# Retention, then a gated linear unit: queries turned as single bf16 tokens or as four-byte words of two

## The chip, the cores and the metric

The kernel runs on one core of one Trainium2 chip. A core has five engines that run side by side, each through its own list of instructions in order: PE (matrix products, with its weight loads shown apart as PEld), DVE (vector), ACT (scalar), POOL (GpSimd) and SP, which here only starts DMAs. They meet through semaphores. The metric is the device time of one run in microseconds (us); lower is better.

## The reference

There are 8 batches, 8 heads, 576 tokens and 64 elements a head. The first half is retention: attention without softmax, with a decay per head.

```python
scores = scale * np.matmul(q, k.transpose(0, 1, 3, 2))
gamma = 1.0 - 2.0 ** (-5.0 - np.arange(H, dtype=np.float32))
Dmat = np.where(rel >= 0, gamma[:, None, None] ** rel[None, :, :], 0.0)
x = np.matmul(scores * Dmat, v)        # then heads side by side: (B, S, 512)
```

The second half takes that x, runs a causal convolution of five taps per channel, and gates a linear layer with it.

```python
gate = 1.0 / (1.0 + np.exp(-causal_conv(x, conv_w)))
out = (gate * (x @ w_val)) @ w_out
```

## The kernel before

The work is cut into 36 chunks of 128 tokens: four full ones for each batch, and after every four batches two "tail" chunks that hold the last 64 tokens of two batches each. The decay is folded into the values (a factor per token, L221) and into the result (L331), so that a chunk needs: scores of keys against queries (`scores`, L273), a product with a causal mask (`masks`, L286), values times masked scores (`values`, L313), plus queries times the state that earlier chunks left (`carried`, L295), and the state's update (`update`, L342, copied out by `take_state`, L356). Two chunks together make a unit for the second half: convolution as products with diagonal matrices (`conv`, L378), `gate`, `value` and `project` (L391 to L420).

PE contracts over partitions, so keys and queries, which arrive with tokens on the partitions, have to be turned: head elements go onto the partitions. For each group of 128 columns (two heads) PE multiplies the data with an identity in its transpose mode and writes the turned tile into PSUM; a copy takes it from there to SBUF. `turn_k` does that for keys, `turn_q` for queries.

Queries of a batch are loaded at once (`load_queries`, L105) as float32, four consecutive tokens to a partition: 128 partitions, 8 heads, 4 tokens `r`, 64 elements. A query job `("batch", b, r)` takes one `r`: `cast_q` (L228) makes it bf16 with 512 elements a partition (POOL, unless another engine is named), and `turn_q` (L252) turns its four groups and copies the result to one quarter of the tile `qtb` of that batch. The tokens of a chunk are therefore ordered by `r` first, and the mask `mask_q` (L160) is stored in that order. Queries of tail chunks have jobs of their own, `("own", t)`.

The order is written out by hand. Each engine runs its instructions in the order in which the program's calls name them. From L448 to L540 stands a prologue for the first chunks; batch 0 is cast at L457 and turned at L461 to L463, batch 1 at L519 and L528 to L531. `keep_warm` issues products that no result uses. Then a loop over slots (L542 to L597): slot `t` loads ahead, casts values for `t + 2` and queries for the jobs of `t + 1`, computes the scores of `t + 1` and the values of `t`, and does half of a unit's second part: convolution and `value` in even slots, `project` in odd ones. The turns of a query job stand between the two `value` or `project` calls (L584), a second job of the same slot after them (L591). Which slot has which job is in `qjobs` (L425 to L432): batch 2 in slots 5 and 6, two jobs each, later batches one job in each of the last four free slots before they are needed.

Turned keys and queries share one PSUM tile, `tps` (pool `ps_t`, one buffer). The prologue also uses tiles `g` of the pool `ps_g`, which has three buffers and otherwise serves the second half.

Of the kernel before, what the change touches and what calls it, by code (L numbers as in the profile page):

```python
# [13 lines left out]
F32 = mybir.dt.float32  # L14
BF16 = mybir.dt.bfloat16
# [6 lines left out]
def kernel(  # L22
# [10 lines left out]
    nc = tc.nc  # L33
    B, H, S, D = q.shape
    DM = moe_w_val.shape[0]
    KC = moe_conv_w.shape[0]
    P = 128
    NP = H // 2
# [5 lines left out]
    RQ = NCH  # L44
# [4 lines left out]
    consts = ctx.enter_context(tc.tile_pool(name="c", bufs=1))  # L49
    half = ctx.enter_context(tc.tile_pool(name="half", bufs=2))  # L50
    bfp = ctx.enter_context(tc.tile_pool(name="bfp", bufs=4))
# [5 lines left out]
    ps_t = ctx.enter_context(tc.tile_pool(name="pst", bufs=1, space=PSUM))  # L57
# [3 lines left out]
    ps_g = ctx.enter_context(tc.tile_pool(name="psg", bufs=3, space=PSUM))  # L61


    chunks = []
# [6 lines left out]
    with tc.manual_schedule():  # L71

        loaded = {}
# [17 lines left out]
        def load_keys(t):  # L91

            kind, b, c = chunks[t]
            kb = bfp.tile([P, H, D], BF16, name="kb", bufs=LA + 3)
            if kind == "full":
                nc.gpsimd.dma_start(out=kb, in_=k[b, :, c * P:(c + 1) * P, :].rearrange("h p d -> p h d"))  # L96
            else:
                for i in range(2):
                    nc.gpsimd.dma_start(out=kb[i * TAIL:(i + 1) * TAIL],
                                        in_=k[b + i, :, c * P:S, :].rearrange("h p d -> p h d"))  # L100
            kbf[t] = kb
# [9 lines left out]
        cwn = consts.tile([KC * NP, P], F32, name="cwn")  # L111
# [30 lines left out]
        for h in range(H):  # L142
# [5 lines left out]
        ident = consts.tile([P, P], BF16, name="ident")  # L148
        nc.gpsimd.memset(ident, 1.0)
        nc.gpsimd.affine_select(ident, ident, pattern=[[-1, P]], base=0, channel_multiplier=1,  # L150
                                compare_op=ALU.is_equal, fill=0.0)

        mask = consts.tile([P, P], BF16, name="mask")
        nc.gpsimd.memset(mask, 1.0)
# [28 lines left out]
        nc.vector.memset(sbd[1], 0.0)  # L183
        for t in xg:
            nc.vector.memset(t[:, :, :, 0:PAD], 0.0)
        identf = consts.tile([32, 32], F32, name="identf")
        nc.vector.tensor_copy(identf, ident[0:32, 0:32])
        id2 = consts.tile([P, 64], F32, name="id2")
        nc.vector.tensor_tensor(id2, ident[:, 0:64], ident[:, 64:128], op=ALU.add)
        mask_t = consts.tile([P, P], BF16, name="maskt")  # L190
# [4 lines left out]

        def prep_conv_weights():
            cps = ps_t.tile([P, KC * NP], F32, name="tps")
            nc.tensor.transpose(cps, cwn, identf[0:KC * NP, 0:KC * NP])
            nc.vector.tensor_copy(cw, cps)

        def prep_diagonals(o, eng):
# [12 lines left out]
        def cast_k(t, copy):  # L214
            kb = bfp.tile([P, H, D], BF16, name="kb", bufs=LA + 3)
            copy(kb, loaded["k", *chunks[t]])  # L216
            kbf[t] = kb

        def cast_v(t, eng=nc.gpsimd):
            vb = bfp.tile([P, H, D], BF16, name="vb")  # L220
            eng.tensor_tensor(vb, loaded["v", *chunks[t]],  # L221
                                    gin[:, chunks[t][2], :].unsqueeze(2).to_broadcast([P, H, D]), op=ALU.mult)
            vbf[t] = vb


        qbf, qtd = {}, {}

        def cast_q(job, copy=nc.gpsimd.tensor_copy):  # L228
            qb = bfp.tile([P, H, D], BF16, name="qb", bufs=5)
            if job[0] == "own":  # L230
                src = loaded["q", *chunks[job[1]]]
            else:
                src = loaded["qb", job[1]][:, :, job[2], :]
            copy(qb, src)  # L234
            qbf[job] = qb

        def turned(src, pool=None):
            ps = pool.tile([P, NP, P], BF16, name="g") if pool else ps_t.tile([P, NP, P], BF16, name="tps")
            flat = src.rearrange("p h d -> p (h d)")
            for pr in range(NP):  # L240
                nc.tensor.transpose(ps[:, pr, :], flat[:, pr * P:(pr + 1) * P], ident)  # L241
            return ps
# [6 lines left out]
            copy(kt, ps)  # L249
            ktd[t] = kt  # L250

        def turn_q(job, copy=nc.scalar.copy, pool=None):  # L252
            ps = turned(qbf[job], pool)
            if job[0] == "own":
                qt = tp_sb.tile([P, NP, P], BF16, name="qt")
                qtd["own", job[1]] = qt
                dst = qt
            else:
                b, r = job[1:]
                if ("batch", b) not in qtd:  # L260
                    qtd["batch", b] = tp_sb.tile([P, NP, RQ, P], BF16, name="qtb", bufs=2)
                dst = qtd["batch", b][:, :, r, :]
            copy(dst, ps)  # L263

        def queries(t, rows, pr):
            kind, b, c = chunks[t]
# [6 lines left out]
        def scores(t, spare=False):  # L273
            kt = ktd[t]
            s = [ps_g.tile([P, NP, P], F32, name="g") if spare else ps_s.tile([P, NP, P], F32, name=f"s{i}")
                 for i in range(2)]
            for pr in range(NP):
                for i in range(2):
                    r = slice(i * 64, i * 64 + 64)
                    nc.tensor.matmul(s[i][:, pr, :], lhsT=kt[r, pr, :], rhs=queries(t, r, pr),  # L280
                                     start=(pr == 0), stop=(pr == NP - 1), skip_group_check=True)
            sps[t] = s
# [12 lines left out]
        def carried(t, spare=False):  # L295

            kind, b, c = chunks[t]
            o = ps_g.tile([P, NP, P], F32, name="g") if spare else ps_o.tile([P, NP, P], F32, name="o")
            ops[t] = o
            rows = slice(0, P)  # L300
            if kind == "full":
                if c:
                    for pr in range(NP):
                        nc.tensor.matmul(o[:, pr, :], lhsT=state[b][:, pr, :], rhs=queries(t, rows, pr),  # L304
                                         start=(pr == 0), stop=False, skip_group_check=True)
            else:
                for pr in range(NP):
                    for i in range(2):
                        cs = slice(i * TAIL, (i + 1) * TAIL)
                        nc.tensor.matmul(o[:, pr, cs], lhsT=state[b + i][:, pr, :], rhs=queries(t, rows, pr)[:, cs],  # L310
                                         start=(pr == 0 and i == 0), stop=False, skip_group_check=True)
# [84 lines left out]
        def value(n, i):  # L396
            vps = ps_g.tile([P, 2, 2 * P], F32, name="g")
            for j in range(2):
                for o in range(NP):
                    nc.tensor.matmul(vps[:, j, :], lhsT=wvb[:, o, 2 * i + j, :], rhs=xs(n, slice(0, P), o, PAD),  # L400
                                     start=(j == 0 and o == 0), stop=(j == 1 and o == NP - 1), skip_group_check=True)
            z = gp.tile([P, 2, 2 * P], BF16, name=f"z{i}")
            nc.vector.tensor_tensor(z, gsb[n][i], vps, op=ALU.mult)  # L403
            zsb[n, i] = z
# [17 lines left out]

        ok = lambda t: 0 <= t < NT
        start_of = {b: t for t, (kind, b, c) in enumerate(chunks) if c == 0}
        qjobs = {5: [("batch", 2, 0), ("batch", 2, 1)], 6: [("batch", 2, 2), ("batch", 2, 3)]}  # L425
        for t, (kind, b, c) in enumerate(chunks):
            if kind == "tail":
                qjobs[t - 2] = [("own", t)]
        for b in range(B - 1, 2, -1):
            fit = [s for s in range(7, start_of[b] - 1) if s not in qjobs][-RQ:]  # L430
            for r, s in enumerate(fit):
                qjobs[s] = [("batch", b, r)]  # L432
        qload = {}
# [4 lines left out]
        v_copy, g_copy, s_copy = nc.vector.tensor_copy, nc.gpsimd.tensor_copy, nc.scalar.copy  # L438
        rhs0 = sbd[0].rearrange("p o j -> p (o j)")

        def keep_warm(n, turn_bank=False):

            idle = ps_t.tile([P, DM], F32, name="tps") if turn_bank else ps_g.tile([P, DM], F32, name="g")
            for _ in range(n):
                nc.tensor.matmul(idle, rhs0[:, 0:P], rhs0, start=True, stop=True)  # L445
# [8 lines left out]
        prep_diagonals(2, nc.gpsimd)  # L454
        prep_diagonals(3, nc.gpsimd)
        keep_warm(7)
        for (r, copy) in ((1, v_copy), (2, s_copy), (0, g_copy), (3, v_copy)):  # L457
            cast_q(("batch", 0, r), copy)
        cast_k(1, g_copy)
        load_keys(3)  # L460
        for (r, copy) in ((1, s_copy), (2, v_copy), (0, s_copy)):  # L461
            turn_q(("batch", 0, r), copy, ps_g)
        turn_q(("batch", 0, 3), v_copy)  # L463
        scores(0)
        masks(0, 0)
        masks(0, 1)
# [49 lines left out]
        update(3)  # L516
        take_state(3)
        keep_warm(3, turn_bank=True)
        for (r, copy) in ((0, g_copy), (1, g_copy), (2, s_copy), (3, g_copy)):  # L519
            cast_q(("batch", 1, r), copy)  # L520
        cast_v(4)
        load_keys(6)
        conv(1)
# [1 line left out]
        gate(1, 1)  # L525
        turn_k(4, s_copy)
        value(1, 0)
        turn_q(("batch", 1, 0), v_copy)  # L528
        turn_q(("batch", 1, 1), s_copy, ps_g)
        turn_q(("batch", 1, 2), v_copy)  # L530
        turn_q(("batch", 1, 3), s_copy, ps_g)  # L531
        carried(4)
        update(4)
        scores(4)
# [7 lines left out]
        for t in range(4, NT + 2):  # L542
            n = t // 2 - 1
# [82 lines left out]
```

## Time and profile before

| | |
|---|---|
| Time, median of three runs | 169.72 us (168.92 to 170.02) |
| Run with the profile | 168.61 us, of which 166.7 us from the first instruction to the last |
| Granted clock of PE, mean | 0.998 of full speed |
| HBM traffic | 30.42 MB read, 9.44 MB written |

The page names every group of instructions by its line, its engine and the tiles that it writes and reads, with its count, its total and mean time, and the idle time of the engine just ahead of it. How these instructions stand in the program for the groups that matter:

| Line | What it is | Count | Mean |
|---|---|---|---|
| L234 | cast of queries of a batch, POOL / DVE / ACT | 28 / 2 / 2 | 620 / 886 / 618 ns |
| L241 | turn of one group of queries or keys, PE | 288 | about 220 ns from start to end, overlapping |
| L263 | copy of turned queries of a batch, ACT / DVE | 28 / 4 | 588 / 425 ns |
| L249 | copy of turned keys, DVE / ACT | 33 / 3 | 423 / 588 ns |
| L221 | values times decay, POOL | 36 | 1046 ns |
| L96 | start of a key load, POOL | 30 | 946 ns |

[...] neighbours overlap, so what a row of them costs PE is read from the distance of their starts, or from the chain of waits.

### The profile page before, as it was taken

To read this page: it belongs to the slowest core of one execution; us is meant where nothing else is said; L and a number is where in the kernel's file an instruction comes from. 1 tells how busy PE (TensorE), PEld (TensorE's weight loads), DVE (VectorE), ACT (ScalarE), POOL (GpSimd) and SP (SyncE) were. 2 spreads that over 40 slices of the span, in tenths; PEclk is the share of its full clock that TensorE was granted. 3 is DMA by queue.
4 is the path that set the end of the run, shared out by engine and by line. 5 is a ranking of instruction groups with operands and counts; after the bars stand their busy time and mean duration, and the time that the engine had idled before them with its cause. 6 is when DMAs were issued, how large, how long until landed. Compare 5 with 4: busy or idle time off the path is not lost.

```text
span 166.7 us, 5543 instructions
## 1 busy us (share of the span) xinstructions
PE 153.5 (92%) x2297; PEld 110.2 (66%) x2297; DVE 114.2 (68%) x217; ACT 89.9 (54%) x183; POOL 99.4 (60%) x132
## 2 busy tenths in 40 slices
PE   6768878799999999999999999999999999999970
PEld 1344656556868777777868686868686877868630
DVE  6784673676677777768677777777777788686330
ACT  6934337446655557474546556565555563554430
POOL 7596999279699378675379286537977462000000
PEclk9999999999999999999999999999999999999999
DMA  5999999998999999999999999999999991303204
GB/s 112 301 264 253 294 213 288 226 162 238 275 263 287 247 236 214 174 258 267 267 163 246 268 274 188 216 285 289 233 259 187 212 236 42 130 0 130 97 33 126
DMA packets 93958, 35.23 MB, mean 211 GB/s; under 512 B 80090, under 2 KB 88814, under 8 KB 93934
## 3 DMA queue, kind: packets, MB, share of 16 engines
q1 hardware_dynamic: 57744, 29.63, 67.7%
q0 software_dynamic: 36000, 4.98, 44.0%
q8 instruction: 18, 0.29, 0.8%
q10 hardware_dynamic: 190, 0.27, 0.6%
q14 instruction: 6, 0.05, 0.1%
HBM read 30.42 MB, written 9.44 MB: 239 GB/s over the span
## 4 chain that ended last, share of the span: by engine, by line
PE 83%; ACT 4%; DVE 3%; POOL 3%; DMA 2%; issue 2%; ACTq 0%; DVEq 0%; POOLq 0%
PE g L400 18%; PE g L411 18%; PE g L385 13%; PE tps L241 10%; PE o L321 7%; PE s L280 7%; PE st L352 4%; PE o L304 3%; DMA fkc<-in_k_dram 2%; PE tps L445 1%; POOL dg L202 1%; ACT qtb L263 1%; DVE p L289 1%; DVE kt L249 1%; ACT ob L414 1%
## 5 line engine op out<-in xcount | busy, mean ns | idle before, releaser
L289 DVE TENSOR_TENSOR p<-s,maskq 128x512 bf16<-128x512 f32 x62 | 42.2, 685 | 17.6 <-PE s L280 17.5
L221 POOL TENSOR_TENSOR vb<-fvc,gin 128x512 bf16<-128x512 f32 x36 | 37.7, 1046 | 22.0 <-DMA fvc<-in_v_dram 9.0
L403 DVE TENSOR_TENSOR z<-gate,g 128x512 bf16<-128x512 f32 x36 | 24.7, 687 | 20.8 <-PE g L400 20.8
L400 PE MATMUL g<-xg,wvb 128*128 128x256 bf16 x288 | 36.9, 273 | 0.0
L411 PE MATMUL g<-wob,z 128*128 128x512 bf16 x144 | 36.5, 379 | 0.3 <-DVE z L403 0.3
L414 ACT COPY ob<-g 128x512 f32<-128x512 f32 x36 | 21.1, 585 | 28.3 <-PE g L411 28.0
L393 ACT ACTIVATE gate<-g 128x512 f32<-128x512 f32 x36 | 19.5, 594 | 19.1 <-PE g L385 19.1
L400 PEld LDWEIGHTS <-wvb 128*128 128x128 bf16 x288 | 26.6, 98 | 3.3 <-issue 0.6
L96 POOL DMA_DIRECT2D kb<-in_k_dram x30 | 28.4, 946 | 0.1
L234 POOL CAST qb<-fqb 128x512 bf16<-128x512 f32 x28 | 17.0, 620 | 13.1 <-DMA fqb<-in_q_dram 13.1
L385 PE MATMUL g<-xg,dg 64*64 64x256 bf16 x720 | 23.2, 271 | 0.0
L363 ACT CAST sbd<-st 64x256 bf16<-64x256 f32 x48 | 17.6, 366 | 8.8 <-PE st L352 8.3
L331 DVE TENSOR_TENSOR xg<-o,gout 128x512 bf16<-128x512 f32 x31 | 21.1, 681 | 1.3 <-PE o L321 1.3
L385 PEld LDWEIGHTS <-dg 64*64 64x64 bf16 x720 | 18.4, 106 | 2.3 <-issue 0.8
L411 PEld LDWEIGHTS <-z 128*128 128x128 bf16 x144 | 12.5, 98 | 10.4 <-DVE z L403 1.2
L263 ACT COPY qtb<-tps 128x512 bf16<-128x512 bf16 x24 | 14.1, 588 | 4.2 <-PE tps L241 4.2
L241 PE MATMUL tps<-ident,kb 128*128 128x128 bf16 x144 | 14.5, 224 | 0.8 <-DVE kb L216 0.8
L280 PE MATMUL s<-qtb,kt 64*128 64x128 bf16 x248 | 12.3, 219 | 2.5 <-DVE kt L249 1.1
L249 DVE COPY kt<-tps 128x512 bf16<-128x512 bf16 x33 | 14.0, 423 | 0.9 <-PE tps L241 0.7
L321 PE MATMUL o<-p,vb 128*64 128x128 bf16 x280 | 14.5, 225 | 0.0
L241 PEld LDWEIGHTS <-qb 128*128 128x128 bf16 x144 | 10.6, 98 | 5.4 <-issue 1.4
L352 PE MATMUL st<-vb,kb 128*128 128x128 bf16 x128 | 12.4, 219 | 0.7 <-POOL vb L221 0.7
(71 smaller groups left out, 142.0 us busy)
## 6 DMA issues: line engine op xcount, KB each, us to landing
fqb<-in_q_dram SPq DMA_DIRECT2D x8, 1024.0 KB, 9.3
fvc<-in_v_dram SPq DMA_DIRECT2D x32, 256.0 KB, 8.8
out_dram<-ob SPq DMA_DIRECT2D x32, 256.0 KB, 5.7
kb<-in_k_dram POOLq DMA_DIRECT2D x30, 128.0 KB, 7.5
wvf<-in_moe_w_val_dram SPq DMA_DIRECT2D x1, 1024.0 KB, 7.4
fqc<-in_q_dram SPq DMA_DIRECT2D x8, 128.0 KB, 5.2
fvc<-in_v_dram SPq DMA_DIRECT2D x8, 128.0 KB, 5.0
out_dram<-ob SPq DMA_DIRECT2D x6, 128.0 KB, 3.3
```

The costliest lines, as they stand in the source:

```text
L96: nc.gpsimd.dma_start(out=kb, in_=k[b, :, c * P:(c + 1) * P, :].rearrange("h p d -> p h d"))
L221: eng.tensor_tensor(vb, loaded["v", *chunks[t]], gin[:, chunks[t][2], :].unsqueeze(2).to_broadcast([P, H, D]), op=ALU.mult)
L241: nc.tensor.transpose(ps[:, pr, :], flat[:, pr * P:(pr + 1) * P], ident)
L280: nc.tensor.matmul(s[i][:, pr, :], lhsT=kt[r, pr, :], rhs=queries(t, r, pr), start=(pr == 0), stop=(pr == NP - 1), skip_group_check=True)
L289: nc.vector.tensor_tensor(p, sps[t][i], m.unsqueeze(1).to_broadcast([P, NP, P]), op=ALU.mult)
L321: nc.tensor.matmul(o[r, pr, :], lhsT=vb[:, 2 * pr + i, :], rhs=pt[t, i][:, pr, :], start=(fresh and pr == 0), stop=(pr == NP - 1), skip_gr ...
L331: nc.vector.tensor_tensor(by_token(x[:, bl, :, PAD + i0:PAD + i0 + P]), ops[t].rearrange("p o (r n) -> p o n r", r=RQ), by_token(gout[:, : ...
L385: nc.tensor.matmul(g[bank][cols, pr, :], lhsT=dg[rows, blk, kk, :], rhs=xs(n, rows, blk, kk), start=(pr == 0 and kk == 0), stop=(pr == 1 a ...
L400: nc.tensor.matmul(vps[:, j, :], lhsT=wvb[:, o, 2 * i + j, :], rhs=xs(n, slice(0, P), o, PAD), start=(j == 0 and o == 0), stop=(j == 1 and ...
L403: nc.vector.tensor_tensor(z, gsb[n][i], vps, op=ALU.mult)
L411: nc.tensor.matmul(o, lhsT=zsb[n, j // 2][:, j % 2, i * P:(i + 1) * P], rhs=wob[:, j, :], start=(j == 0), stop=(j == NP - 1))
L414: nc.scalar.copy(ob, o)
```

## The change

Two bf16 values fit in a four-byte word. The change casts the queries of two tokens of a partition into one tile in which the two tokens' values for the same element lie side by side, looks at that tile as float32, and turns the words: a word keeps its two halves, so that one turn moves two tokens. A batch then has two jobs, `("batch", b, s)`, instead of four, each with four turns of float32 words. The words come out in PSUM with the two tokens interleaved; the copy to `qtb` separates them again, writing each token's values to its own quarter. It is meant to halve the number of query turns on PE.

What goes with it: a float32 identity of full size, `ident_w`, copied by POOL (the small one that DVE made goes, and the turn of the convolution weights uses the new one); in the prologue a cast or a copy can be shared by two engines, each doing one half of the heads; the turned half is copied before the next half is turned. In the loop there is one cast (POOL, 1024 elements a partition) and one copy (ACT, 1024 elements) per job. Jobs of batch 2 stand in slots 5 and 6, one each; later batches use every second of the four slots that they had. Own queries of tail chunks stay in bf16, with a tile name of their own, `qo`.

```diff
+        ident_w = consts.tile([P, P], F32, name="identw")
+        nc.gpsimd.tensor_copy(ident_w, ident)
...
-        identf = consts.tile([32, 32], F32, name="identf")
-        nc.vector.tensor_copy(identf, ident[0:32, 0:32])
...
-        def cast_q(job, copy=nc.gpsimd.tensor_copy):
-            qb = bfp.tile([P, H, D], BF16, name="qb", bufs=5)
+        def cast_q(job, *copies):
...
-                src = loaded["qb", job[1]][:, :, job[2], :]
-            copy(qb, src)
+                qb = bfp.tile([P, H, D, 2], BF16, name="qb", bufs=4)
+                src = loaded["qb", job[1]][:, :, 2 * job[2]:2 * job[2] + 2, :].rearrange("p h r d -> p h d r")
+                copies = copies or (nc.gpsimd.tensor_copy,)
+                hs = H // len(copies)
+                for i, copy in enumerate(copies):
+                    copy(qb[:, i * hs:(i + 1) * hs], src[:, i * hs:(i + 1) * hs])
...
-                b, r = job[1:]
+                b, s = job[1:]
+                ps = pool.tile([P, NP, P], F32, name="g") if pool else ps_t.tile([P, NP, P], F32, name="tps")
+                words = qbf[job].rearrange("p h d r -> p (h d r)").bitcast(F32)
...
-                dst = qtd["batch", b][:, :, r, :]
-            copy(dst, ps)
+                dst = qtd["batch", b][:, :, 2 * s:2 * s + 2, :].rearrange("p o r n -> p o n r")
+                src = ps.bitcast(BF16).rearrange("p o (n r) -> p o n r", r=2)
+                copies = copies or (nc.scalar.copy,)
+                os = NP // len(copies)
+                for i, copy in enumerate(copies):
+                    rows = slice(i * os, (i + 1) * os)
+                    for pr in range(NP)[rows]:
+                        nc.tensor.transpose(ps[:, pr, :], words[:, pr * P:(pr + 1) * P], ident_w)
+                    copy(dst[:, rows], src[:, rows])
...
-        qjobs = {5: [("batch", 2, 0), ("batch", 2, 1)], 6: [("batch", 2, 2), ("batch", 2, 3)]}
+        qjobs = {5: [("batch", 2, 0)], 6: [("batch", 2, 1)]}
...
-            fit = [s for s in range(7, start_of[b] - 1) if s not in qjobs][-RQ:]
+            fit = [s for s in range(7, start_of[b] - 1) if s not in qjobs][-RQ::2]
...
-        for (r, copy) in ((1, v_copy), (2, s_copy), (0, g_copy), (3, v_copy)):
-            cast_q(("batch", 0, r), copy)
+        cast_q(("batch", 0, 0), v_copy, s_copy)
+        cast_q(("batch", 0, 1), v_copy, g_copy)
...
-        for (r, copy) in ((1, s_copy), (2, v_copy), (0, s_copy)):
-            turn_q(("batch", 0, r), copy, ps_g)
-        turn_q(("batch", 0, 3), v_copy)
+        turn_q(("batch", 0, 0), v_copy, s_copy, pool=ps_g)
+        turn_q(("batch", 0, 1), v_copy, s_copy, pool=ps_g)
...
-        for (r, copy) in ((0, g_copy), (1, g_copy), (2, s_copy), (3, g_copy)):
-            cast_q(("batch", 1, r), copy)
+        cast_q(("batch", 1, 0), g_copy)
+        cast_q(("batch", 1, 1), s_copy, g_copy)
...
-        turn_q(("batch", 1, 0), v_copy)
-        turn_q(("batch", 1, 1), s_copy, ps_g)
-        turn_q(("batch", 1, 2), v_copy)
-        turn_q(("batch", 1, 3), s_copy, ps_g)
+        turn_q(("batch", 1, 0), v_copy, s_copy)
+        turn_q(("batch", 1, 1), v_copy, s_copy, pool=ps_g)
```

More of the change, by code (lines that the diff above doesn't have):

```diff
@@ L197, in prep_conv_weights @@
             cps = ps_t.tile([P, KC * NP], F32, name="tps")
-            nc.tensor.transpose(cps, cwn, identf[0:KC * NP, 0:KC * NP])
+            nc.tensor.transpose(cps, cwn, ident_w[0:KC * NP, 0:KC * NP])
             nc.vector.tensor_copy(cw, cps)
@@ L226 @@
         qbf, qtd = {}, {}
-        def cast_q(job, copy=nc.gpsimd.tensor_copy):
-            qb = bfp.tile([P, H, D], BF16, name="qb", bufs=5)
+        def cast_q(job, *copies):
             if job[0] == "own":
-                src = loaded["q", *chunks[job[1]]]
-            else:
-                src = loaded["qb", job[1]][:, :, job[2], :]
-            copy(qb, src)
+                qb = bfp.tile([P, H, D], BF16, name="qo", bufs=2)
+                nc.gpsimd.tensor_copy(qb, loaded["q", *chunks[job[1]]])
+            else:
+                qb = bfp.tile([P, H, D, 2], BF16, name="qb", bufs=4)
[4 more added lines that the diff above has]
+                    copy(qb[:, i * hs:(i + 1) * hs], src[:, i * hs:(i + 1) * hs])
             qbf[job] = qb
@@ L250, in turn_k, with turn_q @@
             ktd[t] = kt
-        def turn_q(job, copy=nc.scalar.copy, pool=None):
-            ps = turned(qbf[job], pool)
+        def turn_q(job, *copies, pool=None):
             if job[0] == "own":
+                ps = turned(qbf[job])
                 qt = tp_sb.tile([P, NP, P], BF16, name="qt")
                 qtd["own", job[1]] = qt
-                dst = qt
+                nc.scalar.copy(qt, ps)
             else:
-                b, r = job[1:]
+                b, s = job[1:]
+                ps = pool.tile([P, NP, P], F32, name="g") if pool else ps_t.tile([P, NP, P], F32, name="tps")
+                words = qbf[job].rearrange("p h d r -> p (h d r)").bitcast(F32)
                 if ("batch", b) not in qtd:
                     qtd["batch", b] = tp_sb.tile([P, NP, RQ, P], BF16, name="qtb", bufs=2)
-                dst = qtd["batch", b][:, :, r, :]
-            copy(dst, ps)
+                dst = qtd["batch", b][:, :, 2 * s:2 * s + 2, :].rearrange("p o r n -> p o n r")
[7 more added lines that the diff above has]
+                    copy(dst[:, rows], src[:, rows])
         def queries(t, rows, pr):
```

## The prediction

> **What bounds the kernel now.** I read the page's shares first, then the table by stage, then the chain of waits, then groups by shape, last the timeline of the two places where query words are turned before the loop.
>
> ```profile
> PE 153.5 (92%) x2297; PEld 110.2 (66%) x2297; DVE 114.2 (68%) x217; ACT 89.9 (54%) x183; POOL 99.4 (60%) x132
> PE 83%; ACT 4%; DVE 3%; POOL 3%; DMA 2%; issue 2%; ACTq 0%; DVEq 0%; POOLq 0%
> ```
>
> PE is 83% of the chain that ended last. The table by stage (us; busy of each engine) says where:
>
> ```profile
> 60.00:90.00 30.00, 30.00 (x492) 22.51 (x491) 22.99 (x42) 16.45 (x36) 21.01 (x27) 1.00 1.26 223
> 90.00:120.00 30.00, 30.00 (x462) 22.49 (x464) 22.22 (x38) 17.94 (x40) 19.91 (x25) 1.00 1.35 253
> ```
>
> From 60 to 120 us PE has no gap: there only PE's own time counts. The chain between 69 and 72 us prices the work concerned:
>
> ```profile
> 69.70 0.86 PE g L411 x4
> 70.56 0.22 PE tps L241 x4
> 70.78 0.86 PE g L411 x4
> ```
>
> The middle line is one query job: four turns, 0.22 us of PE, 56 ns each. The copy behind it (L263) is not in the chain, since PE goes on with L411. Before about 33 us it is otherwise: PE waits for copies.
>
> ```profile
> 29.38 0.38 PE tps L241 x4
> 29.76 0.24 PE g L241 x4
> 30.00 0.02 issue
> 30.02 0.59 ACT qtb L263
> 30.62 0.04 issue
> 30.66 0.43 PE s L280 x8
> ```
>
> Batch 1's last copies are waited for by the scores, and batch 0's at 10 us likewise. The groups that price the new forms:
>
> ```profile
> L234 POOL CAST qb<-fqb 128x512 bf16<-128x512 f32 x28 | 17.0, 620 | 13.1 <-DMA fqb<-in_q_dram 13.1
> L263 ACT COPY qtb<-tps 128x512 bf16<-128x512 bf16 x24 | 14.1, 588 | 4.2 <-PE tps L241 4.2
> L249 DVE COPY kt<-tps 128x512 bf16<-128x512 bf16 x33 | 14.0, 423 | 0.9 <-PE tps L241 0.7
> L337 DVE TENSOR_TENSOR xg<-o,gout 128x256 bf16<-128x256 f32 x8 | 3.0, 414 | 0.0
> L331 DVE TENSOR_TENSOR xg<-o,gout 128x512 bf16<-128x512 f32 x31 | 21.1, 681 | 1.3 <-PE o L321 1.3
> L160 POOL COPY maskq<-mask 128x128 bf16<-128x128 bf16 x1 | 0.8, 761 | 0.0
> L596 POOL COPY maskt<-mask 128x128 bf16<-128x128 bf16 x1 | 0.3, 283 | 0.0
> L198 PEld LDWEIGHTS tps<-identf,cwn 20*128 20x128 f32 x1 | 0.2, 175 | 0.8 <-DVE kt L249 0.8
> ```
>
> The last is the only float32 turn there is; maskq is the only POOL copy with a scattered side, maskt its plain twin.
>
> [...] L198's load took 175 ns where the bf16 loads of that moment (4.8 to 5.5 us) took 129. [...]
>
> **The change, part by part.**
>
> *Turns in the loop.* Batches 2 to 7 have 24 jobs of 0.22 us: 5.3 us of PE, all on the path. In place come 12 jobs of four float32 turns. Low bound: same step as bf16, 56 ns, 12 × 0.22 = 2.7 us. High bound: four times that, 12 × 0.90 = 10.7 us. [...] I take 115 ns a turn, 0.46 us a job[...]. Added to it: in the old program the loads of a job run ahead (L241's loads for queries start 0.1 to 0.2 us before the turns, 70.18 against 70.40 us). [...] 0.1 us a job. 12 × 0.56 = 6.7 us, minus 5.3: **+1.4 us** (-2.7 to +6.6).
>
> *Two jobs in one slot at slots 5 and 6 go.* Their second turn waited for the first one's copy, and the scores for the second (0.23 us at 44.95): **-0.3 us**.
>
> *Copies in the loop.* ACT: (588-366)/256 = 0.87 ns an element from L263 and the 256-wide L363 (366 ns), so 1024 elements take 1.03 us, once where 588 stood twice. It holds the only tps tile 0.45 us longer, but the next turn into it is a slot's scores and values away, and the 8 matmuls of L411 and L304/L352 lie between. Behind it on ACT stand the second projection's copy and the next state copies; ACT is 54% busy and that copy's bank is wanted again only after the next convolution. Nothing on the path.
>
> *Casts on POOL.* From 283 and 609 ns for 128 and 512 elements: 0.85 ns an element and 0.17 fixed. Now 1024 elements, read in pairs 256 bytes apart. Low: 1.04 us. [...] High, by maskq: (761-174)/128 = 4.6 ns, 4.9 us. I take 2.6. Behind it queue the key load and the value cast, about 2.0 us a slot (946 and 1046 ns); two slots last 8.05 us (from 70.78 to 78.82). 2.6 + 4.0 = 6.6 fits in, and the first cast of batch 3 ends 2.3 us before its turn at 46.72, others 2 to 5. Hidden; at 4.9 us it isn't.
>
> *Batch 1.* Each job is turned in two halves with copies by DVE and then ACT into the same tiles, and in the new program the second half's turn waits for DVE's copy of the first. A half has 512 elements, written at a step, so DVE takes 681 ns (L331), not 425. Behind the waiting turn on PE stand the state update and the scores, for which DVE's masks wait. From 28.5: two turns 0.4 (with latency), DVE 0.7, two turns 0.4, then the second tile's DVE 0.9 with its turns, turns 0.4, ACT 0.6: the scores at 32.0 instead of 30.66, **+1.3 us**.
>
> *Batch 0.* Same shape. Before, scores(0) ran at 10.65 and the state update at 12.12, held by POOL. After: DVE's copy waits behind its second cast until 9.6, then 0.7, turns 0.4, turns and DVE 0.9, turns 0.4, ACT 0.6: scores at 12.6, and the key turn, update, second scores behind them on PE. They regain part, since they waited before: **+1.3 us**. [...]
>
> Of these 2.6 us some 0.4 come back where PE waits for key DMAs at 34 us and for copies at 38: **+2.2 us** (1.0 to 4).
>
> *Rest.* The float32 identity adds a POOL copy like maskt, 0.28 us before 4 us, and removes DVE's 585 ns one; neither engine is waited for there. The casts of own queries stay.
>
> Sum: 169.7 + 1.4 - 0.3 + 2.2 = 173.0.
>
> **The rivals.** *Cheap turns.* 56 ns a turn: -2.7 - 0.3 + 2.2 = 168.9, no change. For: [...] weight loads may hide behind turns as bf16's do (PEld 66% busy). Against: the 175 ns load. With a prologue of only +1.0, which a DVE copy at 425 ns and quick regain would give, **faster**, 167.7. *Dear turns.* [...] 224 ns and lead-in, 169.7 + 6.6 - 0.3 + 2.2 = 178.2. For: L198 with 20 columns took 288 ns[...]; a single one can't say whether its load or its stream was long. *POOL becomes the bound.* 4.9-us casts make 8.9 us per 8.05-us pair: eight pairs × 0.85, and the first cast about 2 us late against batch 3's turn, some 8 to 9 us over 173: 181. For: maskq. Against: its step is on the write side[...].
>
> **How the numbers follow.** Forecast 0.47, dear turns 0.17, POOL 0.08, cheap turns and no change 0.18, faster 0.10. Predicted 173.0. Range 168.2 to 179.0, leaving out POOL and the faster case, 0.18. Faster by 1% (below 168.0) 0.13, with a tail of the no-change case; within 0.20; slower 0.67.
>
> **What would show it.** Four float32 turns in the chain at 0.4 to 0.6 us where 0.22 stood (0.22: cheap; 0.9: dear). L277's copies at 1.03 us on ACT and 0.68 on DVE. L239 on POOL near 2.6 us, with PE still without gaps from 60 to 120. First scores near 12.6 us, first L411 some 2 us later than 33.5. I am wrong if the prologue does not shift, or if the loop gets shorter by over 2 us.

## The result, and the profile after

The changed kernel takes 217.8 us (217.62 to 218.42), the kernel before beside it 169.3: ratio 1.287, interval 1.280 to 1.294. The forecast was 173.0 us, the range 168.2 to 179.0. The direction was right, but the time lies far above the range: the loss is 48 us, where the steps of the forecast add up to 3.3.

Page of the changed kernel, shares and chain:

```profile
PE 165.9 (77%) x2233; PEld 115.1 (53%) x2233; DVE 122.2 (57%) x216; ACT 137.8 (64%) x171; POOL 100.6 (47%) x120
PEclk9975799757998899999999979999999999999999
PE 46%; ACT 24%; issue 16%; DVE 6%; DMA 5%; SPq 1%; ACTq 0%; DVEq 0%
ACT qtb L277 11%; PE g L414 11%; PE g L425 10%; ACT ob L428 6%; DVE qtb L277 5%; PE tps L246 4%; PE g L399 4%; PE o L335 4%; PE s L294 4%; DMA fvc<-in_v_dram 4%; ACT gate L407 3%; ACT sbd L377 3%; PE st L366 2%; DMA fkc<-in_k_dram 2%; PE g L459 1%
```

PE was 83% of the chain and is 46% of a longer one; ACT went from 4% to 24%, led by L277, the copy of turned words. ACT is busy for 137.8 us instead of 89.9, although it has fewer instructions. PE's granted clock, 1.00 everywhere up to 140 us before, is now 0.84, 0.90, 0.74 and 0.91 in the four stretches of 20 us up to 80 us. The groups by shape (busy us, mean ns, idle before) name the cause:

```profile
L277 ACT COPY qtb<-tps 128x1024 bf16<-128x1024 bf16 x12 | 56.6, 4719 | 0.3 <-PE tps L276 0.3
L277 DVE COPY qtb<-g 128x512 bf16<-128x512 bf16 x3 | 7.2, 2416 | 1.9 <-PE g L276 1.7
L239 POOL CAST qb<-fqb 128x1024 bf16<-128x1024 f32 x13 | 16.3, 1255 | 1.2 <-DMA fqb<-in_q_dram 1.2
L276 PE MATMUL tps<-identw,qb 128*128 128x128 f32 x52 | 8.5, 286 | 3.1 <-DVE qtb L277 2.5 <-ACT kt L254 0.5
```

A copy of 1024 values takes ACT 4.72 us, not 1.03, and a half takes DVE 2.42 us, not 0.68: some 4.4 ns a value on both engines (an estimate, with the 0.14 us fixed cost that the prediction's two ACT groups imply). The mask copy on POOL in the kernel before had nearly that price, 4.6 ns. How that reaches PE, in the timeline from 62 us (start, length, in brackets the idle time before):

```profile
62.79 4.69 ACT L277 COPY qtb<-tps 128x1024 bf16<-128x1024 bf16 x1
63.93 0.09 PEld L294 LDWEIGHTS <-kt 64*128 64x128 bf16 x1
...
67.53 0.40 PE L294 MATMUL s<-qtb,kt 64*128 64x128 bf16 x8 [3.53 <-ACT qtb L277]
...
71.36 4.71 ACT L277 COPY qtb<-tps 128x1024 bf16<-128x1024 bf16 x1 [0.27 <-PE tps L276]
75.58 0.92 ACT L428 COPY ob<-g 128x512 f32<-128x512 f32 x1
76.13 0.38 PE L246 MATMUL tps<-ident,kb 128*128 128x128 bf16 x4 [1.57 <-ACT qtb L277]
```

The scores of batch 2's first chunk have their keys loaded at 63.9 and wait 3.5 us for the copy. Nine microseconds later it is the next key turn that waits, for the one PSUM tile that the copy still reads; and the copy of a projection (L428) comes only after it on ACT. In the waits of the whole run (us, times, longest):

```profile
PE tps L246 <- ACT qtb L277: 19.0, 11, 1.9
PE g L276 <- DVE qtb L277: 7.8, 3, 2.6
PE s L294 <- ACT qtb L277: 7.5, 3, 3.5
PE tps L276 <- DVE qtb L277: 2.5, 1, 2.5
```

The first line is the loop, the key turn behind 11 of the 12 jobs; the second and fourth are the halves in the prologue; the third is scores, two of its three waits in the prologue. Together they are 36.8 us, and PE's idle time grew by as much (50.0 of 215.9 us, 13.2 of 166.7 before). The other 12.4 us of the longer span are busy time of PE (165.9 instead of 153.5), with 64 matmuls fewer. The lower granted clock can lengthen it: at 68.56 us, with 0.57 granted from 68 to 72, four products of L425 take 1.91 us, where four of the same products took 1.03 before, at 1.00. So can rows of matmuls that are broken up, since a record is longer than the step of a row (272 ns for one float32 turn, 110 from one to the next in the bench below). How much each has of the 12.4 us was not separated. Most of it goes when the copy is fast: in the first experiment below PE is busy 156.4 us.

### The profile page after: what moved, and what is told of

The parts are those of the page before. It is cut to its first block, busy times and chain, and to the rows that moved or that the text cites. A ratio compares the mean times of both kernels' runs of the same rounds, so it can differ in the third digit from the quotient of the medians.

```text
span 215.9 us, 5405 instructions
## 1 busy us (share of the span) xinstructions
PE 165.9 (77%) x2233; PEld 115.1 (53%) x2233; DVE 122.2 (57%) x216; ACT 137.8 (64%) x171; POOL 100.6 (47%) x120
## 4 chain that ended last, share of the span: by engine, by line
PE 46%; ACT 24%; issue 16%; DVE 6%; DMA 5%; SPq 1%; ACTq 0%; DVEq 0%
ACT qtb L277 11%; PE g L414 11%; PE g L425 10%; ACT ob L428 6%; DVE qtb L277 5%; PE tps L246 4%; PE g L399 4%; PE o L335 4%; PE s L294 4%; DMA fvc<-in_v_dram 4%; ACT gate L407 3%; ACT sbd L377 3%; PE st L366 2%; DMA fkc<-in_k_dram 2%; PE g L459 1%
## 5 line engine op out<-in xcount | busy, mean ns | idle before, releaser
L277 ACT COPY qtb<-tps 128x1024 bf16<-128x1024 bf16 (+1 forms) x13 | 59.0, 4542 | 3.8 <-PE tps L276 3.8
L428 ACT COPY ob<-g 128x512 f32<-128x512 f32 x36 | 24.9, 692 | 31.2 <-PE g L425 31.2
L414 PE MATMUL g<-xg,wvb 128*128 128x256 bf16 x288 | 38.4, 280 | 2.5 <-ACT gate L407 2.1
L425 PE MATMUL g<-wob,z 128*128 128x512 bf16 x144 | 37.9, 390 | 0.3 <-DVE z L417 0.3
L414 PEld LDWEIGHTS <-wvb 128*128 128x128 bf16 x288 | 28.2, 100 | 9.7 <-issue 6.0
L246 PEld LDWEIGHTS <-kb 128*128 128x128 bf16 x144 | 9.5, 100 | 25.9 <-issue 21.9
L294 PE MATMUL s<-qtb,kt 64*128 64x128 bf16 x248 | 13.5, 229 | 8.2 <-ACT qtb L277 7.5
L425 PEld LDWEIGHTS <-z 128*128 128x128 bf16 x144 | 13.4, 100 | 11.3 <-DVE z L417 1.2
L239 POOL CAST qb<-fqb 128x1024 bf16<-128x1024 f32 (+1 forms) x15 | 17.9, 1201 | 1.2 <-DMA fqb<-in_q_dram 1.2
L294 PEld LDWEIGHTS <-kt 64*128 64x128 bf16 x288 | 8.8, 98 | 13.4 <-issue 8.9
```

Of the source, the lines that this page charges most:

```text
L277: copy(dst[:, rows], src[:, rows])
L425: nc.tensor.matmul(o, lhsT=zsb[n, j // 2][:, j % 2, i * P:(i + 1) * P], rhs=wob[:, j, :], start=(j == 0), stop=(j == NP - 1))
L428: nc.scalar.copy(ob, o)
```

## The experiments

The ratios below are to the kernel before, run on the same chip.

**Runs of 128, same elements, other order.** The copy's loops change places: a run of one token is written, every second value is read.

```diff
-                dst = qtd["batch", b][:, :, 2 * s:2 * s + 2, :].rearrange("p o r n -> p o n r")
-                src = ps.bitcast(BF16).rearrange("p o (n r) -> p o n r", r=2)
+                dst = qtd["batch", b][:, :, 2 * s:2 * s + 2, :]
+                src = ps.bitcast(BF16).rearrange("p o (n r) -> p o r n", r=2)
```

> The changed kernel, with the copy of the turned words in another order of the same elements: for each token of the pair a run of 128 values is written, and every second bf16 value of PSUM is read (before: every value read in turn, written to the two runs by turns, 256 bytes apart). Theory W, 2-byte writes that jump cost some 4.4 ns each (from 4719 ns for 1024 on ACT and 2416 ns for 512 on DVE): the jumps go, ACT's copy falls to about 1.03 us, DVE's half to 0.68, and the time to what the prediction's other steps give, 171 to 175 us. Rival R, it is the reading of half words out of PSUM: the copies stay at 4.7 and 2.4 us or get worse, and the time stays at 210 to 225 us. Rival P, the turns and the halves that wait for each other are what costs: copies fall, but the time stays above 190 us.

172.45 us, ratio 1.018 (1.014 to 1.021). The groups, and the chain where a job stands in the loop:

```profile
L277 ACT COPY qtb<-tps 128x1024 bf16<-128x1024 bf16 x12 | 12.2, 1017 | 0.5 <-PE tps L276 0.5
L277 DVE COPY qtb<-g 128x512 bf16<-128x512 bf16 x3 | 2.1, 692 | 1.6 <-PE g L276 1.6
```

```profile
65.98 0.86 PE g L425 x4
66.84 0.44 PE tps L276 x4
67.28 0.86 PE g L425 x4
```

Same bytes, same engines, same PSUM reads but for their order: 45 of the 48 us are gone. The copies cost what the prediction put down. A job costs PE 0.44 us, with nothing before or behind it; two bf16 jobs cost 0.45. Theory W, jumping writes, stands; R, reads of half words, and P, turns and halves, fall as causes of the great loss.

**Words copied as words.** As above, but `qtb` keeps pairs and the copy moves 512 float32.

```diff
+                dst = qtd["batch", b].rearrange("p o s n r -> p o s (n r)")[:, :, s, :].bitcast(F32)
+                src = ps
...
-            return qtd["batch", b][rows, pr, :, c * P // RQ:(c + 1) * P // RQ]
+            return qtd["batch", b][rows, pr, :, c * P // RQ:(c + 1) * P // RQ, :].rearrange("p s n r -> p s (n r)")
```

> The changed kernel, with the words copied as they are: 512 float32 words a job, written in one run per group, so that a query tile keeps the two tokens side by side; the scores take their queries in that order, and mask and result follow it (the result's factor step takes two instructions of 256 elements instead of one of 512 on DVE). Theory W: ACT's copy 0.59 us, as for 512 elements in the kernel before, DVE's half 0.41 us; the prologue gets shorter than in the run with runs of 128 by about 0.3 us for each of four DVE halves and 0.2 for each ACT half, so 170 to 173 us. Rival P: above 190 us.

172.12 us, 1.015 (1.009 to 1.021): within the expectation. ACT's copy is 591 ns, DVE's half 420.

**The loop alone, the prologue alone.** Words for some batches, bf16 for the others.

```diff
+        WORDS = (2, 3, 4, 5, 6, 7)     # the other run: (0, 1)
...
+                if b not in WORDS:
+                    ps = turned(qbf[job], pool)
...
+                    (copies or (nc.scalar.copy,))[0](qtd["batch", b][:, :, s, :], ps)
+                    return
```

> Words, copied in runs of 128, for batches 2 to 7 only; batches 0 and 1 are cast, turned and copied as in the kernel before. What the loop costs alone. Theory W with the trace after: four float32 turns measured 0.60 us from the first start to the last end with 273 ns for one, so 109 ns a step and 0.44 us a job of PE, against 0.45 for two bf16 jobs; with some lead-in of 0.1 us on 12 jobs +1 us, minus 0.3 for the double jobs: 169.3 to 171 us. Rival P: the loop is dear by its turns, above 175 us.

> Words, copied in runs of 128 and in halves as in the changed kernel, for batches 0 and 1 only; batches 2 to 7 as in the kernel before. What the prologue costs alone. Theory W with the prediction's step: +1.0 to +4.0 us, 170.5 to 173 us, and with the run of the loop alone it adds up to the run of both within 1 us. Rival: the prologue's delay is swallowed by waits for DMAs before 38 us, within 0.5 us of the kernel before.

The loop alone: 169.27 us, ratio 0.9997 (0.997 to 1.002), nothing won and nothing lost. The prologue alone: 174.1 us, 1.026 (1.021 to 1.030), above the expectation. The two sum to +4.8 us and both together cost +3.1, so the sum was missed by 1.7 us, more than the 1 us allowed. In the profile of the prologue run ACT's first query cast begins at 9.04 us, held 1.42 us by its load; with runs of 128 for all batches it began at 7.53. That load alone does not explain it: with words copied as words the cast began at 9.03 us, and that kernel took 172.12. The rest of the difference stays open.

**Jumps without words.** The kernel before, bf16 turns and four jobs, its copy going through its elements with the group innermost: a write lands 1024 bytes after the last, and a read of PSUM 256 bytes after the last.

```diff
-            copy(dst, ps)
+            copy(dst.rearrange("p o n -> p n o"), ps.rearrange("p o n -> p n o")) if job[0] != "own" else copy(dst, ps)
```

> The kernel before, with its bf16 turns and its four jobs a batch; only the order in which the copy of turned queries of a batch goes through its elements is changed: group innermost, so that each 2-byte write lands 1024 bytes after the last (and each read of PSUM 256 bytes). No words at all. Theory W: 512 jumping writes cost what they cost after the change, 2.4 us a copy on ACT and DVE, 24 of them in the loop, 57 us of ACT as after the change; PE waits for the copies as there, and the time rises to 200 to 225 us. Rival T, the turns of words are part of the loss: with bf16 turns the time stays under 185 us even if the copy is slow.

197.95 us, 1.169 (1.162 to 1.176). ACT's copies are 2450 ns (24 in the loop, 58.8 us). The time is 2 us under the range given, well over the rival's: a slow copy alone, with no word in the kernel, costs 29 us. Reads jump here too; that the price is the writes' is seen in the bench below, where a copy with a step of 16 bytes on the write side alone takes 2419. Its 58.8 us of ACT are a little more than the 56.6 after the change, and the loss is smaller; that shorter copies hold the tile and the queue for less time each would explain it, but was not tried by itself.

**The bench.** Copies and turns behind the kernel's own work, in a single run: each copy below is one record.

```diff
+        for i in range(8):
+            nc.tensor.transpose(bt2[0:32, i % 4, :], wsrc[:, i * P:i * P + 32], idw)            # L608
+        for i in range(8):
+            nc.tensor.transpose(bt3[:, i % 4, 0:32], wsrc[0:32, i * P:(i + 1) * P], idw[0:32, 0:32])  # L611
...
+            copy(sb[:, 0:512], h1[:, 0:512])                                       # L623, runs
+            copy(v2(sb[:, 0:1024], 2)[:, :, 0], h1[:, 0:512])                      # L624, step 4 bytes
+            copy(v2(sb[:, 0:2048], 4)[:, :, 0], h1[:, 0:512])                      # L625, 8
+            copy(v2(sb[:, 0:4096], 8)[:, :, 0], h1[:, 0:512])                      # L626, 16
+            copy(v2(sb, 16)[:, :, 0], h1[:, 0:256])                                # L627, 32
+            copy(v2(sb, 32)[:, :, 0], h1[:, 0:128])                                # L628, 64
+            copy(v2(sb, 64)[:, :, 0], h1[:, 0:64])                                 # L629, 128
+            copy(sb[:, 0:512], v2(h1, 2)[:, :, 0])                                 # L630, step on the read side
+            copy(sb[:, 0:512].rearrange("p (r n) -> p n r", r=2), v2(h1[:, 0:512], 2))   # L631, two runs by turns
+            copy(sb[:, 0:512].rearrange("p (r n) -> p n r", r=2), v2(sa[:, 0:512], 2))   # L632, the same, read from SBUF
+            copy(sb.bitcast(F32)[:, 0:512].rearrange("p (r n) -> p n r", r=2), v2(p1, 2))  # L633, the same, float32
+            copy(v2(sb.bitcast(F32), 4)[:, :, 0], p1)                              # L634, float32, step 16 bytes
...
+            copy(sb[:, 0:512].rearrange("p (r n x) -> p n r x", r=2, x=4), h1[:, 0:512].rearrange("p (n r x) -> p n r x", r=2, x=4))  # L637, by turns, four values at a time
...
+        nc.gpsimd.tensor_copy(sb[:, 0:512].rearrange("p (r n) -> p n r", r=2), v2(sa[:, 0:512], 2))  # L639
```

> The kernel before, with a bench after its own work: four rows of eight float32 turns (128 x 128; 32 columns loaded and 128 streamed; 128 loaded and 32 streamed; 128 x 128 again), then copies of one kind each on ACT and on DVE, and six on POOL; their lines in the trace are read one by one. Turns: if the load of 128 float32 columns sets the 109 ns, the step falls for 32 loaded columns to about 56 ns[...]; if the stream sets it, the other way round. Copies of 512 bf16 values, theory W: runs written and every second value read 0.59 us on ACT and 0.68 on DVE; two runs written by turns 2.4 us, out of PSUM and out of SBUF alike. Open, and told apart here: whether it is the jump or the size of 2 bytes (float32 values written to two runs by turns: 0.6 to 0.7 us if the size, 2.4 if the jump), and from which step on (4, 8, 16, 32, 64, 128 bytes). POOL: the same form 512 x 4.6 + 170 = 2.5 us by its mask copy.

Groups by line. POOL's rows and L632 read SBUF, the others PSUM, `h1` as bf16 and `p1` as float32:

```profile
L639 POOL COPY sb<-sa 128x512 bf16<-128x512 bf16 x1 | 2.4, 2439 | 0.1
...
L626 ACT COPY sb<-g 128x512 bf16<-128x512 bf16 x1 | 2.4, 2419 | 0.0
L626 DVE COPY sb<-g 128x512 bf16<-128x512 bf16 x1 | 2.4, 2419 | 0.0
L631 DVE COPY sb<-g 128x512 bf16<-128x512 bf16 x1 | 2.4, 2415 | 0.0
...
L632 DVE COPY sb<-sa 128x512 bf16<-128x512 bf16 x1 | 1.5, 1454 | 0.0
L625 ACT COPY sb<-g 128x512 bf16<-128x512 bf16 x1 | 1.3, 1291 | 0.0
...
L627 ACT COPY sb<-g 128x256 bf16<-128x256 bf16 x1 | 1.2, 1227 | 0.0
...
L634 ACT COPY sb<-g 128x512 f32<-128x512 f32 x1 | 1.1, 1054 | 0.0
...
L624 ACT COPY sb<-g 128x512 bf16<-128x512 bf16 x1 | 0.7, 737 | 0.0
...
L630 DVE COPY sb<-g 128x512 bf16<-128x512 bf16 x1 | 0.7, 692 | 0.0
...
L630 ACT COPY sb<-g 128x512 bf16<-128x512 bf16 x1 | 0.6, 586 | 0.0
L623 ACT COPY sb<-g 128x512 bf16<-128x512 bf16 x1 | 0.6, 585 | 0.6 <-DVE sa L620 0.6
...
L623 DVE COPY sb<-g 128x512 bf16<-128x512 bf16 x1 | 0.4, 425 | 19.3 <-ACT sb L637 19.3
L637 DVE COPY sb<-g 128x512 bf16<-128x512 bf16 x1 | 0.4, 425 | 0.0
```

A read step of 4 bytes is free on ACT (586 against 585) and costs DVE 0.27 us (692 against 425). The write side is dearer: less 0.14 us fixed, a 2-byte value costs ACT 1.2 ns at a step of 4 bytes, 2.2 at 8, 4.4 at 16 and 4.2 at 32. From there to 128 bytes it stays between 4.2 and 4.7 (L628, 713 ns for 128 values, and L629, 443 for 64). DVE's rows out of PSUM are the same within 10 ns, and POOL's at 4 and 16 bytes (751 and 2445 ns) are close to them.

It isn't one price for every write that jumps, though. Float32 values that jump cost 1.75 to 1.8 ns (1038 ns for L633, 1054 for L634, less 144, over 512), not 4.4 and not free, between the two answers that were set down beforehand. Bf16 values written by turns to two places, four at a time, cost no more than in order (L637, 425 on DVE and 585 on ACT). So in these rows a jump costs less as more bytes land together: 4.4 ns a value with 2 bytes, 1.75 to 1.8 with 4, nothing extra with 8. And the source counts on DVE: the two runs by turns, expected alike out of PSUM and SBUF, take it 2415 ns out of PSUM and 1454 out of SBUF, while ACT takes 2412 and 2446. What in the hardware sets these prices stays open.

The turns, in the timeline:

```profile
161.82 1.04 PE L605 MATMUL g<-idw,wvb 128*128 128x128 f32 x8
162.70 1.04 PE L608 MATMUL g<-idw,wvb 128*32 128x128 f32 x8
163.66 0.68 PE L611 MATMUL tps<-idw,wvb 32*128 32x32 f32 x8
```

With 272 ns for one, a full turn and one that loads 32 columns both step by (1.04-0.272)/7 = 110 ns; with 32 columns streamed (222 ns for one) it is 65 ns. PE ran at its pace of the kernel before: five products of L411 just ahead of the turns, at 160.75 us, took 1.24 us, where four took 1.03 before: with 379 ns for one, 215 and 217 ns a step. In these rows the stream sets the step, not the load (the third row also has only 32 partitions). The first of the two answers, by the load, is refuted.

**Whole jobs in the prologue.** With runs of 128, and then with words copied as words:

```diff
-        turn_q(("batch", 0, 0), v_copy, s_copy, pool=ps_g)
-        turn_q(("batch", 0, 1), v_copy, s_copy, pool=ps_g)
+        turn_q(("batch", 0, 0), v_copy, pool=ps_g)
+        turn_q(("batch", 0, 1), s_copy, pool=ps_g)
...
-        turn_q(("batch", 1, 0), v_copy, s_copy)
-        turn_q(("batch", 1, 1), v_copy, s_copy, pool=ps_g)
+        turn_q(("batch", 1, 0), v_copy)
+        turn_q(("batch", 1, 1), s_copy, pool=ps_g)
```

> The kernel of the run with runs of 128, with one change in the prologue: each job of batches 0 and 1 is turned at once and copied by one engine (DVE the first job, ACT the second) instead of in two halves by both. No turn waits for a copy then. If the waits between the halves are what the prologue cost: first scores at about 11 us instead of 12.0 to 12.7, batch 1's about 1.2 us earlier, and 169.3 to 171 us. If it is the casts or the words themselves: 172 to 173 us, as with halves.

> Words copied as words (512 float32 a job, queries kept in pairs) and each job of the prologue copied whole by one engine. ACT 0.59 us and DVE 0.68 us a job, beside each other. If both the writes and the waits between halves are gone with that, the prologue is at least as short as before (scores 0.2 to 0.4 us earlier), the loop costs PE 0.44 us a job against 0.45 for two, and the time is 168 to 169.5 us; if words have another cost on PE, 170 to 172.

169.44 us, 1.0015 (0.9985 to 1.0044), and 169.13 us, 0.9977 (0.9949 to 1.0005). The 3 us of the prologue go with the turns that waited for the other half's copy. The granted clock does not account for them. With halves and runs of 128 it is 0.84 from 12 to 34 us, but PE is slow for a while with whole jobs too: rows of eight products take 0.61 to 0.64 us at 14.36 and 16.83 us with halves, and at 11.96, 13.79, 16.37 and 18.20 us with whole jobs, where in both they take 0.40 to 0.41 between 20 and 24 us. And the runs of whole jobs with a mean clock of 0.978 to 0.980 took 169.44 to 170.16 us, where halves took 172.33 and more at 0.968 to 0.978. One sign did not come as expected: the first scores ran at 11.96 us, not 11, behind a query load that held ACT's first cast until 8.82; batch 1's came at 33.0 instead of 34.9. With both costs gone the words are level with the kernel before.

**Halves in tiles of their own.** Words as words, halves as in the changed kernel, each half in a PSUM tile of its own.

```diff
+                    if i:
+                        src = ps = (pool2 or ps_g).tile([P, NP, P], F32, name="tps" if pool2 else "g")
...
-        turn_q(("batch", 0, 1), v_copy, s_copy, pool=ps_g)
+        turn_q(("batch", 0, 1), v_copy, s_copy, pool=ps_g, pool2=ps_t)
```

> Words copied as words, halves by DVE and ACT in the prologue as in the changed kernel, but each half turned into a PSUM tile of its own, so that no turn waits for a copy of the other half. The copies of halves took 0.42 and 0.37 us where whole jobs take 0.69 and 0.59. Expected if the waits between halves are the prologue's cost: first scores at 10.5 to 11 us, 168 to 169.2 us, level with or just under the kernel before; if halves cost in another way, 170 to 172 as with words in halves in one tile.

169.45 us, 0.999 (0.996 to 1.002), a little over the range given: level again, so it is the wait between halves and not the halving.

**How the loss splits.** Jumps in the loop only.

```diff
+                if not copies:
+                    dst, src = dst.rearrange("p o r n -> p o n r"), src.rearrange("p o r n -> p o n r")
```

> The changed kernel with its jumping copy in the loop only; in the prologue the copies write runs of 128. How the loss splits. From the two traces: the stretch from the first product of the second half's last step (L425) to the end is 165.0 us in the changed kernel (50.9 to 215.9) and 132.7 with runs (38.1 to 170.8), so the loop's jumps are worth 32 us and the prologue's 13: 204 to 206 us. Rival: the loop hides a part of the prologue's delay, or the other way round, and the two don't add up: below 198 or above 211.

205.1 us, 1.210 (1.203 to 1.218), as worked out. So, taken away in this order: 217.8 - 205.1 = 12.7 us are jumps in the prologue, 205.1 - 172.45 = 32.6 us jumps in the loop, and 172.45 - 169.3 = 3.1 us all the rest of the change.

## Why the prediction was right or wrong

*The step that failed: "Copies in the loop".* It took 0.87 ns an element from copies that write in runs and put 1.03 us and "nothing on the path" beside it. The copy writes by turns to two runs 256 bytes apart, and took 4.72 us. The same term is in "Batch 1" and "Batch 0", where DVE's half was put at 681 ns and took 2.42 us. The run with runs of 128 gives that one term the cost that was put down, and the time is 172.45 us, close to the forecast's 173.0; that this is so close is in part luck, since two of the other terms missed in opposite directions (below). What the runs show in place of "nothing on the path" is a copy that holds PE up: in the loop by the single turned tile (19.0 us) and by scores (3.5), in the prologue by the halves (10.3) and by scores (3.9), and a little by ACT's queue (2.1 us of waits for `gate`, against none before).

The number was on the table. The mask copy's 4.6 ns an element was taken for a price of POOL, and the rival built on it put it on POOL's cast, whose step is on the read side, and noted as much ("Against: its step is on the write side"). It was not carried to the one new instruction that does write at a step. The 681 ns of L331 that stood in its place reads by a step and writes in order. Nor does L331 beside L249 show what a step costs DVE, since L331 reads float32; the bench's 692 and 425 ns, both bf16, do.

*Turns in the loop.* 115 ns was taken and 110 measured, 0.44 us a job in the chain. The 115 was the author's estimate, and so was the factor four of the high bound: no row of the trace before shows either. The prediction left open whether L198's load or its stream was long; in the bench it is the stream that sets the step. (With runs of 128 one float32 load took 140 ns in the loop, and the turns still followed each other at 110: the loads hide.) The lead-in of 0.1 us a job, also an estimate that no row showed, does not show in the chain. The run with words in the loop alone is level with the kernel before (-0.1 us), where the two steps for the loop added up to +1.1.

*Prologue.* +2.2 us forecast. With the copies at their forecast price the whole change costs 3.1 us and the loop nothing, so some 3 us, inside the bounds of 1.0 to 4; by itself it measured 4.8, outside them, and in the trace with runs of 128 the first projection comes at 38.1 us instead of 33.4, 4.7 later where some 2 were put down. This step was too small while the loop's was too large. It also has no term for the granted clock, which was 0.84 from 12 to 34 us in that trace and 1.00 from 12 to 33 us in the trace of the kernel before. The mechanism, turns of a half that wait for the copy of the other, is shown by the two runs that take the wait away in different ways and are level with the kernel before.

*POOL.* 1.25 us a cast, near the low bound of 1.04; the 2.6 us that were taken between the two bounds, the author's estimate, shown by no row of the trace before, did not come at reads in pairs 256 bytes apart. Hidden, as argued; the rival of POOL as the bound is out, and so are dear turns (110 ns, not 224). *Cheap turns* is out as well.

## What to carry to other kernels

When a copy rearranges, put the step on the read side and the runs on the write side: same bytes, 1.0 us against 4.7 on ACT here. On DVE the read step has a price too, 692 ns against 425, but far below the 2415 of the write step. Price a new instruction by a row with the same access on the same side and the same memory to read from; here that told more than a row of the same engine. And an engine that is half idle is no shelter for a slow instruction, if what it reads is the only buffer of the engine that sets the end.

## What was not expected of the hardware

Writes of 2 bytes at a step of 16 bytes cost 4.4 ns each on ACT (2419 ns for 512), on POOL (2445) and on DVE out of PSUM (2419); by turns to two runs DVE took 2415 ns for 512 out of PSUM and 1454 out of SBUF. Float32 writes that jump cost 1.75 to 1.8 ns (1038 and 1054 ns for 512 on ACT), and four bf16 values at a time nothing more than in order (585 ns on ACT, 425 on DVE); a step of 4 bytes on the read side cost ACT nothing (586 ns against 585). Float32 turns step by 110 ns for 128 columns, twice the 56 of bf16, so that a word of two values is turned in the time of two values: there was no PE time to win.
